# Fused bucketed attention and expert layer: block fills, routing operations, first weight buffer and last-pair order changed

## The chip, the cores and the metric

The kernel runs on one core of a Trainium2 chip. The metric is device microseconds (us) of one execution. The kernel before takes 723.25 us, the median of three runs (722.49 to 725.14).

## The reference

Two layers follow each other. The first is attention over 4 batches, 8 heads, 768 tokens and a head width of 64, in which a query sees a key only if both fall into the same of 64 buckets (six signs of random projections). The second sends each of the 3072 tokens (width 512) to one of 8 experts.

```python
q_bits = (np.einsum('bhsd,dk->bhsk', q, proj) > 0)
k_bits = (np.einsum('bhsd,dk->bhsk', k, proj) > 0)
mask = q_bucket[:, :, :, None] == k_bucket[:, :, None, :]
scores = np.where(mask, scale * (q @ k.T), -1e9)
attn = exp(scores - max) / (sum + 1e-9);  x = attn @ v      # then heads side by side: (3072, 512)

logits = x @ w_gate;  expert_idx = argmax(logits)            # first of equal ones
gate_w = softmax(logits)[expert_idx]
y = relu(x @ w1[expert_idx]) @ w2[expert_idx]
out = gate_w[:, None] * y
```

## The kernel before

**Pairs.** Attention goes over 16 pairs of heads, g = 0 to 15, four to a batch. A pair has 12 units of 128 queries (six score tiles to a head). A unit is a score on TensorE (`S`, lines 297 and 299), a minimum with eviction on VectorE (`R`, line 307) and an exponential on ScalarE (`X`, line 313). The probabilities of half of the units are transposed on TensorE (`T`, line 327) and evicted by ScalarE or VectorE (`E`, lines 377 and 375). Those of the other half are transposed in 32x32 blocks on VectorE (`D`, `blocks`, line 349). When the sixth of these is done, 16 DMAs on SP's queue put the blocks into place (`pt`, line 355), which the text calls the pair's **exchange**. `V` multiplies with the values (line 387), `O` evicts that, `K` is the product with the gate columns and an identity (line 407), `L` its eviction into the token rows `xr` (line 417). A minus behind a step means the pair before. So `V0-` of the next pair is what reads an exchange.

**The order of the work** is written out by hand. `HEAD` is pair 0, `PLAN` pairs 1 to 14 and `LAST` pair 15 with the first part of the expert layer. Each word issues its instructions on all engines and queues in program order, and every engine takes its own in that order.

**Empty blocks.** The sorted token rows lie in `sorted_rows`, one stretch for each expert. `fill(e)` (line 147) writes 512 empty rows (1156 KB) for expert e on SP's queue: for e up to 5 from the tile `C["empty"]`, for 6 and 7 by copying rows of expert 0. Blocks 0, 1 and 2 are issued in pair 0, and blocks 3 to 7 in step `I` of pairs 1 to 5, ahead of that pair's exchange.

**Routing.** `route` (line 427) finds each token's expert and slot, batch by batch, in pieces that the `R` steps of later pairs issue behind their own eviction. Batches 0 to 2 are routed whole (six tiles, in pairs 5 and 6, 9 and 10, 13 and 14). Batch 3 is routed in two halves, `r0` and `r1`, in `LAST`. Each has a matmul with a triangle of ones (line 458) that needs the one-hot experts (line 453). `scatter` (line 487) then writes the token rows by indirect DMA from GpSimd's (POOL's) queue.

**Weights.** The first expert's weights are split in two parts of lower precision in 16 pieces on POOL (`weights` and `weight_half`; lines 662 and 663, 906 and 912), four to a chunk. The chunks' buffers are the attention's own (`HOME`): w0 is also where the blocks of pair 14 wait for their exchange, w3 that of pair 13, w2 and w1 hold the last pair's queries and keys. `x`, `g`, `h` transpose the first expert's first 256 rows and split them (lines 749 to 753), `m` is the first product (`mm1`, line 770).

Of the kernel before, what the change touches and what calls it, by code (L numbers as in the profile page):

```python
# [12 lines left out]
OP = mybir.AluOpType  # L13
AX = mybir.AxisListType

B, H, S, D = 4, 8, 768, 64
# [3 lines left out]
NG = B * NP  # L20
# [11 lines left out]
M0 = float(2 ** 34)  # L32
# [22 lines left out]
def lsh_attention_moe(ctx, tc, qk, qk2, v, proj, wg, w1, w1p, w2, out):  # L55
    nc = tc.nc
# [88 lines left out]
    def fill(e):  # L145

        nc.sync.dma_start(xs[e * ROW:e * ROW + FILL].rearrange("(p j) w -> p j w", p=128),
                          C["empty"][:, 0:1].to_broadcast([128, FILL // 128, RW]) if e < 6 else
                          xs[:FILL].rearrange("(p j) w -> p j w", p=128))
# [190 lines left out]
    def blocks(i):  # L340

        g, r = divmod(i, 12)
        c, w = divmod(r, 2)
        if g not in ZT:
            ZT[g] = moe.tile([128, 4, 3, 2, NT * 32], F32, name="w0" if g == NG - 2 else "w3" if g % 2 else "w2"), []
        z, turned = ZT[g]
        turned.append(r)
        e = PP.pop(i).rearrange("p h c -> p (h c)").rearrange("p (k g j) -> p g k j", g=4, j=32)
        nc.vector.transpose(z[:, :, c, w].rearrange("p g (k i) -> p g k i", i=32), e)  # L349
        if len(turned) == 6:  # L350
            pt = pt_tile(2 * g)
            for r in range(4):
                for a in range(4):
                    q = (a + r) % 4
                    nc.sync.dma_start(pt[32 * q:32 * q + 32, a].rearrange("p t s k i -> p (t s k i)"),  # L355
                                      z[32 * a:32 * a + 32, q].rearrange("p c w x -> p (c w x)"))
            del ZT[g]

    def trans_ev(c, k, vec):

# [63 lines left out]
    def bc(ap):  # L424
        return ap[:, :, None].to_broadcast([128, ap.shape[1], E])

    def route(b, hfs):

        nt = 3 * len(hfs)
        l = wk.tile([128, 2, 2 * 3, E], F32, name="rl")  # L430
        lg, eq = l[:, 0, :nt], l[:, 1, :nt]
        f = wk.tile([128, 3, 2 * 3], F32, name="rf")
        mx, fi, sm = f[:, 0, :nt], f[:, 1, :nt], f[:, 2, :nt]
        oh = C["oh"] if nt > 3 else C["ohs"][:, hfs[0]]
        ex = C["ex"][:, 3 * hfs[0]:3 * hfs[0] + nt]
        dsc = C["desc"][:, None, :].to_broadcast([128, nt, E])
        many = nt > 3
        for i, hf in enumerate(hfs):
            nc.vector.tensor_reduce(lg[:, 3 * i:3 * i + 3], XR[b, hf][:, :, :GC].rearrange("p t (a x e) -> p t e a x", a=NP, e=E)[:, :, :, :, 0:PW // E:PW // E - 1], axis=AX.XY, op=OP.add)
            if many:  # L440
                yield
        nc.vector.tensor_reduce(mx, lg, axis=AX.X, op=OP.max)
        nc.vector.tensor_tensor(lg, lg, bc(mx), op=OP.subtract)
        if many:
            yield
        nc.vector.tensor_scalar(eq, lg, 0.0, None, op0=OP.is_equal)
        nc.vector.tensor_tensor(eq, eq, dsc, op=OP.mult)
        yield
        nc.vector.tensor_reduce(fi, eq, axis=AX.X, op=OP.max)
        nc.vector.tensor_tensor(eq, dsc, bc(fi), op=OP.subtract)  # L450
        if many:
            yield
        nc.vector.tensor_scalar(oh[:, :nt], eq, 0.0, None, op0=OP.is_equal)
        yield
        nc.scalar.activation(ex[:, :, 0:E], lg, AF.Exp)
        yield
        p = ps.tile([128, 512], F32, name="t", bufs=2)
        nc.tensor.matmul(p[:, :(nt + 1) * E], C["tri"], oh, start=True, stop=False)

        for t in range(nt):  # L460
            nc.tensor.matmul(p[:, (t + 1) * E:(nt + 1) * E], C["ones"], oh[:, t:t + 1, :].to_broadcast([128, nt - t, E]),
                             start=False, stop=(t == nt - 1))
        yield
        pb = wk.tile([128, 2 * 3 + 1, E], F32, name="pb")
        nc.vector.tensor_tensor(pb[:, :nt + 1], p[:, :(nt + 1) * E].rearrange("p (t e) -> p t e", e=E),
                                C["base"][:, None, :].to_broadcast([128, nt + 1, E]), op=OP.add)
        C["base"] = pb[:, nt]
        pb = pb[:, :nt]
        yield
        nc.vector.tensor_tensor(pb, pb, oh[:, :nt], op=OP.mult)  # L470
        slot = wk.tile([128, 2 * 3], I32, name="slot")
        with nc.allow_low_precision("whole numbers below 2**24"):
            nc.vector.tensor_reduce(slot[:, :nt], pb, axis=AX.X, op=OP.add)
        yield
        nc.vector.tensor_reduce(sm, ex, axis=AX.X, op=OP.add)
        for i, hf in enumerate(hfs):
            nc.vector.reciprocal(XR[b, hf][:, :, GC], sm[:, 3 * i:3 * i + 3])
            SL[b, hf] = slot[:, 3 * i:3 * i + 3]
        yield
# [15 lines left out]
    def go(r, n):  # L495
        for _ in range(n):
            next(r, None)
# [134 lines left out]


    CH, RAW = {}, {}
    HOME = "w0", "w3", "w2", "w1", "w4", "w5"
    P2 = {}

    def raw_load(c, a):
# [16 lines left out]
    def chunk_part(c, a):  # L655

        if a == 0:
            s = c % 6
            CH[c] = (moe if s < 4 else P2["p"]).tile([128, 2, 4, 512], F32R, name=HOME[s])
        w, r = CH[c], RAW[c, a // 2][:, a % 2]  # L660
# [118 lines left out]
    M1 = {}  # L779
# [115 lines left out]
    def weight_half(op, x):  # L895
# [35 lines left out]
    """.split()  # L931

    LAST = """
        S5 R5 S10 T31- R10 T30- S1 E31a- T32- nP tP nP tP E30a- E32a- X5 S0 S4 R4 X4 nP tP M1- R1 X1 V1- O1- T20 E20a
        R0 S2 nP T21 E21v T22 E22v R2 S3 X0 T00 E00a T01 E01a tP R3 S9 X2 T02 E02v R9 X9 S6 R6 X6 K1- L1- V0- O0- K0--
        L0-- S11 M0- S7 X3 T10 E10a M0 T11 E11v X10 S8 nP tP nP tP K0- L0- T12 E12a R8 R7 X8 X7 V0 O0 T31 E31a T30
        E30a T32 E32a R11 T40 E40a T41 E41v T42 E42v X11 T51 E51a M1 T50 T52 E50a K0 E52a V1 O1 L0 r0 r0 r0 r0 r0 r0
        K1 L1 r1 r1 r1 r1 r1 r1 r0 c0 r1 c1 x0 g0 h0 nP tP nP tP x2 g2 h2 m5 m3 u3 d3 u5 d5 m1 u1 d1 m0 u0 d0 m2 u2 d2
        m7 u7 d7 m4 u4 m6 u6 d6 d4
    """.split()  # L940

    SCAT = {}
# [1 line left out]
    steps = dict.fromkeys(range(B - 1), 0)  # L944

    def on(b, n):
        for _ in range(n):
            next(routes[b], None)
            steps[b] += 1

    def route_step(g, w, k):

        b, q = divmod(g - NP, NP)
        if 0 <= b < B - 1 and w[0] == "R" and q == 1 and {(g - 2, "L0"), (g - 2, "L1")} <= DONE and steps[b] < 7:
            if b not in routes:
                routes[b] = route(b, (0, 1))
            on(b, 1)
        if 0 <= b < B - 1 and q == 2:
            if w == "G":
                on(b, 9 - steps[b])  # L960
            elif w[0] == "R" and 9 <= steps[b] < 11:
                on(b, 1)
        s = {7: (0, 0), 8: (0, 1), 11: (1, 0), 12: (1, 1), 14: (2, 0)}.get(g)
        if w == "P7" and s:
            go(scatter(*s), 4)
        if g == NG - 1 and w[0] == "R" and k < 3:
            if k == 0:
                SCAT[0] = scatter(2, 1)
            go(SCAT[0], 1)
            if k == 2:  # L970
                rows(0)
# [27 lines left out]
    DONE = set()  # L999

    def step(g, w):

        n = g - w.count("-")
        w = w.rstrip("-")
# [5 lines left out]
        op, x = w[0], w[1:]  # L1010
# [12 lines left out]
            trans(6 * n + int(x[0]), int(x[1]))  # L1023
        elif op == "I":
            loads(n)
            if 0 < n < 6:
                fill(n + 2)
        elif op == "D" and n:
            blocks(12 * n + int(x))
        elif op == "E":  # L1030
# [63 lines left out]
    for g in range(NG):  # L1094
        peaks, since = 0, 0
        for w in HEAD if g == 0 else LAST if g == NG - 1 else PLAN:
            if w == "G":
                route_step(g, w, 0)
                since = 1
            step(g, w)  # L1100
            if g == 0 and w in ("z0", "z1"):
                fill(int(w[1]))
            if g == 0 and w == "w":
                fill(2)
            if w == "P7":
                route_step(g, w, 0)
            if w[0] == "R":
                route_step(g, w, peaks)
                if g == NG - 2 and 0 < since < 7 and steps[2] >= 9:
                    next(pick, None)  # L1110
                    since += 1
                    if since == 5:
                        raw_load(0, 0)
                        raw_load(0, 1)
                peaks += 1
            if g == NG - 1 and w == "c1":
                GT[0] = moe.tile([128, 4], F32, name="gate", bufs=3)
                nc.vector.tensor_copy(GT[0][:, :2], XG[0][:, :, GC])
                tokens(0)
# [30 lines left out]
    for n in range(1, len(PH)):  # L1150
        c0 = 4 * (PH[n][0] + 1)
# [91 lines left out]
```

## Time and profile before

| | |
|---|---|
| median of three runs | 723.25 us |
| the profiled execution | 723.71 us, span 721.9 us, mean granted TensorE clock 0.991 |
| TensorE (PE) busy | 97% of the span |
| VectorE (DVE), ScalarE (ACT), GpSimd (POOL) busy | 63%, 60%, 65% |
| chain that ended last, by engine | PE 82%, issue 5%, DVE 4%, DMA 3%, POOL 2%, ACT 2% |
| idle TensorE, by what ended it, in all | routing's one-hot (line 453) 5.3 us; row eviction (line 417) 3.6 us; line 387 after the eviction of line 377 3.0 us; masks 1.3 us |

With one engine busy nearly all the time, what remains is in the gaps of that engine. They are looked for in the list of waits and then, one by one, in order of time. A granted clock of 1.00 is 2.4 GHz and one of 0.50 is 1.2 GHz.

### The profile page before, as it was taken

Reading aid. Unit: us, or ns where it says so; the run is one execution under the profiler, and the core shown is the slowest. Engines: PE = TensorE matmul, PEld = TensorE weight load, DVE = VectorE, ACT = ScalarE, POOL = GpSimd, SP = SyncE. Lnnn points to the kernel's source line nnn. Section 1 sums busy time; section 2 is a strip of 40 time slices with the busy share of each in tenths; the row PEclk is TensorE's granted clock in tenths of the full one; section 3 lists DMA queues with packets and bytes.
Section 4 is the critical chain, followed back from the end, with each engine's and each line's share of the span. In section 5 each row is a group of like instructions: output and inputs, shape, how many; then the busy total and the mean of one; then the engine's idle time right before and its main releaser. Section 6 shows DMA issues by size and latency. Waiting matters only on the chain.

```text
span 721.9 us, 12253 instructions
## 1 busy us (share of the span) xinstructions
PE 697.0 (97%) x4219; PEld 570.3 (79%) x4219; DVE 456.6 (63%) x931; ACT 434.6 (60%) x864; POOL 468.0 (65%) x505
## 2 busy tenths in 40 slices
PE   8899999899999999999999699999999999999997
PEld 5777767767786768676876498899999999989896
DVE  8878777977878887788864723631757634262521
ACT  7988778677888788886865213544444444443320
POOL 7957745655887458874907854675666676768532
PEclk9999999999999999999999899999999999999999
DMA  7719878966787457864864236583637395747201
GB/s 287 209 33 263 204 219 203 230 186 161 207 218 218 132 140 221 226 204 115 242 187 164 94 132 172 196 231 126 166 123 189 132 124 188 193 148 201 88 11 40
DMA packets 64528, 123.09 MB, mean 171 GB/s; under 512 B 15331, under 2 KB 29027, under 8 KB 64400
## 3 DMA queue, kind: packets, MB, share of 16 engines
q1 hardware_dynamic: 56736, 103.17, 51.7%
q0 software_dynamic: 7584, 19.10, 8.9%
q8 instruction: 34, 0.56, 0.3%
q14 instruction: 30, 0.25, 0.1%
q10 hardware_dynamic: 144, 0.02, 0.0%
HBM read 65.75 MB, written 26.33 MB: 128 GB/s over the span
## 4 chain that ended last, share of the span: by engine, by line
PE 82%; issue 5%; DVE 4%; DMA 3%; POOL 2%; ACT 2%; SPq 2%; POOLq 0%; ACTq 0%
PE s L770 18%; PE t L387 17%; PE s L807 10%; PE s L297 8%; PE s L299 8%; PE t L327 8%; PE s L827 8%; PE t L407 3%; SPq L355 2%; DMA w<-masks 1%; PE t L254 1%; PE s L836 1%; ACT e L313 1%; DVE e L307 1%; DMA pt<-w 1%
## 5 line engine op out<-in xcount | busy, mean ns | idle before, releaser
L307 DVE TENSOR_SCALAR_CACHE_REDUCE e<-s 128x768 f32<-128x768 f32 x192 | 178.6, 953 | 65.6 <-PE s L299 56.6
L313 ACT ACTIVATE e<-e,m 128x768 f32<-128x768 f32 x192 | 177.9, 930 | 18.8 <-DVE e L307 16.6
L666 POOL TENSOR_TENSOR w<-raw,w 128x512 fp32r<-128x512 f32 x112 | 144.5, 1316 | 38.6 <-ACT w L665 38.1
L387 PE MATMUL t<-pt,vt 128*64 128x384 f32 x768 | 130.9, 490 | 4.0 <-ACT pt L377 3.0
L770 PE MATMUL s<-xh,w 128*128 128x456 f32 (+6 forms) x672 | 126.8, 346 | 0.0
L770 PEld LDWEIGHTS s<-xh,w 128*128 128x128 f32 x672 | 119.2, 188 | 3.1
L387 PEld LDWEIGHTS t<-pt,vt 128*64 128x64 f32 x768 | 53.6, 137 | 66.9 <-issue 55.2
L786 DVE SCALAR_TENSOR_TENSOR hh<-s,hh 128x256 fp32r<-128x256 f32 (+7 forms) x64 | 35.5, 555 | 109.3 <-ACT hh L784 103.9
L327 PE MATMUL t<-ident,e 128*128 128x128 f32 x648 | 92.7, 275 | 4.8 <-DVE xr L417 3.6
L377 ACT ACTIVATE pt<-t 128x512 f32<-128x512 f32 (+1 forms) x150 | 84.2, 582 | 17.9 <-PE t L327 16.4
L327 PEld LDWEIGHTS t<-ident,e 128*128 128x128 f32 x648 | 76.8, 141 | 13.1 <-ACT pt L377 4.0
L784 ACT ACTIVATE hh<-s 128x256 fp32r<-128x256 f32 (+7 forms) x64 | 31.4, 490 | 89.9 <-PE s L770 86.5
L349 DVE STREAM_TRANSPOSE w<-e 128x768 f32<-128x768 f32 x84 | 79.2, 966 | 0.2 <-ACT e L313 0.2
L807 PE MATMUL s<-hh,w 128*128 128x456 f32 (+3 forms) x384 | 74.9, 355 | 0.0
L807 PEld LDWEIGHTS s<-hh,w 128*128 128x128 f32 x384 | 71.1, 188 | 2.6
L665 ACT ACTIVATE w<-raw 128x512 fp32r<-128x512 f32 x112 | 66.3, 622 | 3.6 <-DMA raw<-in_w1p_dram 3.6
L843 POOL DMA_INDIRECT out_dram<-y,ix x26 | 25.9, 995 | 62.1 <-DVE y L841 30.9
L297 PE MATMUL s<-w 80*128 80x384 f32 x192 | 56.0, 373 | 2.2 <-DMA w<-masks 1.3
L827 PE MATMUL s<-w,hh 128*128 128x512 f32 (+1 forms) x240 | 56.4, 394 | 0.0
L297 PE MATMUL s<-qk 80*128 80x384 f32 x192 | 54.8, 367 | 0.0
L827 PEld LDWEIGHTS s<-w,hh 128*128 128x128 f32 (+1 forms) x240 | 44.6, 187 | 10.5
L299 PE MATMUL s<-w 128*128 128x384 f32 x192 | 50.0, 342 | 0.0
(205 smaller groups left out, 1000.1 us busy)
## 6 DMA issues: line engine op xcount, KB each, us to landing
pt<-w SPq DMA_DIRECT2D x224, 144.0 KB
raw<-in_w_dram SPq DMA_DIRECT2D x36, 512.0 KB
raw<-in_w1p_dram SPq DMA_DIRECT2D x28, 512.0 KB
xd<-in_qk_dram SPq DMA_DIRECT2D x14, 768.0 KB
sorted_rows<-xr SPq DMA_DIRECT2D x6, 1156.0 KB
vt<-in_v_dram SPq DMA_DIRECT2D x16, 384.0 KB
masks<-bits POOLq DMA_DIRECT2D x14, 192.0 KB, 3.8
sorted_rows<-sorted_rows SPq DMA_DIRECT2D x2, 1156.0 KB
```

The lines of the kernel that those rows point to most:

```text
L297: nc.tensor.matmul(p[:, a, :HALF], k[0:80, 2, c], k[0:80, 3, n], start=i >= 4, stop=i < 4)
L299: nc.tensor.matmul(p[:, a, :HALF], k[:, 0, c], k[:, 1, n], start=i < 4, stop=i >= 4)
L307: nc.vector.tensor_scalar(e, SC.pop(i)[:, :, :HALF], CEIL, None, op0=OP.min, op1=OP.min, accum_out=m)
L313: nc.scalar.activation(e, e, AF.Exp, bias=m, scale=-1.0, accum_out=SM[g, hf][:, t, s:s + 1])
L327: nc.tensor.transpose(o[:, j, w], e[w][:, kt // 3, (kt % 3) * 128:(kt % 3) * 128 + 128], ident)
L349: nc.vector.transpose(z[:, :, c, w].rearrange("p g (k i) -> p g k i", i=32), e)
L377: nc.scalar.activation(o, x, AF.Copy)
L387: nc.tensor.matmul(p[s * 64:(s + 1) * 64, :HALF], VT[g][:, kt, s, :], PT[u][:, :, :, s, kt].rearrange("p a t i -> p t a i"), start=(kt == ...
L666: nc.gpsimd.tensor_tensor(w[:, 1, a], r, w[:, 0, a], op=OP.subtract)
L770: nc.tensor.matmul(p[:, :c], w[:, a, d, fs], x[:, b, d, :c], start=(k == 0), stop=(k == 11))
L807: nc.tensor.matmul(p[:, :c], w[:, a, f % 4, ms], h[b][:, f, :c], start=(k == 0), stop=(k == 23))
L827: nc.tensor.matmul(p[:pw], HH[n][b][:, f, i:i + pw], w[:, a, f % 4], start=(k == 0), stop=(k == 23))
```

## The change

Four things change.

1. `fill(2)` leaves pair 0 and `fill(3)` to `fill(7)` leave step `I`. Instead `fill(g + 1)` is issued behind the 16 exchange DMAs of pairs 1 to 6.
2. `route` compares the logits with their maximum directly, and the order number with the found one directly, instead of a subtraction and a comparison with zero each. The subtraction that the exponential needs comes later, on POOL for batches 0 to 2 and on VectorE for batch 3. The pieces are one fewer for batches 0 to 2, and the counts in `route_step` and in the loop follow.
3. `HOME` begins with w3 instead of w0: the first chunk of weights goes to w3 and the second to w0.
4. `LAST` has a new order.

```diff
@@ blocks
             del ZT[g]
+            if g < 7:
+                fill(g + 1)
@@ route
         nc.vector.tensor_reduce(mx, lg, axis=AX.X, op=OP.max)
-        nc.vector.tensor_tensor(lg, lg, bc(mx), op=OP.subtract)
+        nc.vector.tensor_tensor(eq, lg, bc(mx), op=OP.is_equal)
         if many:
             yield
-        nc.vector.tensor_scalar(eq, lg, 0.0, None, op0=OP.is_equal)
         nc.vector.tensor_tensor(eq, eq, dsc, op=OP.mult)
-        yield
+        if not many:
+            yield
         nc.vector.tensor_reduce(fi, eq, axis=AX.X, op=OP.max)
-        nc.vector.tensor_tensor(eq, dsc, bc(fi), op=OP.subtract)
         if many:
             yield
-        nc.vector.tensor_scalar(oh[:, :nt], eq, 0.0, None, op0=OP.is_equal)
+        nc.vector.tensor_tensor(oh[:, :nt], dsc, bc(fi), op=OP.is_equal)
+        (nc.gpsimd if many else nc.vector).tensor_tensor(lg, lg, bc(mx), op=OP.subtract)
         yield
@@
-    HOME = "w0", "w3", "w2", "w1", "w4", "w5"
+    HOME = "w3", "w0", "w2", "w1", "w4", "w5"
@@ LAST
-        S5 R5 S10 T31- R10 T30- S1 E31a- T32- nP tP nP tP E30a- E32a- X5 S0 S4 R4 X4 nP tP M1- R1 X1 V1- O1- T20 E20a
...
+        S0 S1 R0 R1 T31- E31a- T30- E30a- M0- S5 R5 S6 X0 T32- E32a- nP tP X5 S4 R4 X4 X1 R6 X6 K0-- L0-- M1- V1- O1-
...
@@ step
             loads(n)
-            if 0 < n < 6:
-                fill(n + 2)
@@ loop
-            if g == 0 and w == "w":
-                fill(2)
```

SP's queue from pair 1's exchange to the loads behind pair 2's, before and now (`pt` is the exchange, `xd` and `vt` are loads of queries, keys and values, `sorted_rows` a block):

```order
L355 DMA pt<-w_521 32x1152 x16
L80 DMA xd<-in_qk_dram 128x1536
L84 DMA vt<-in_v_dram 128x768
L147 DMA sorted_rows<-xr 512x1x578
L355 DMA pt<-w_786 32x1152 x16
L80 DMA xd<-in_qk_dram 128x1536
```

```order
L355 DMA pt<-w_520 32x1152 x16
L147 DMA sorted_rows<-xr 512x1x578
L80 DMA xd<-in_qk_dram 128x1536
L84 DMA vt<-in_v_dram 128x768
L355 DMA pt<-w_785 32x1152 x16
L147 DMA sorted_rows<-xr 512x1x578
L80 DMA xd<-in_qk_dram 128x1536
```

The block stands behind the exchange instead of ahead of it, and the load of the next queries and keys stands behind both, as it did.

POOL's queue in pair 5, before and now (`qk`, `xd` are the next pair's operands, `masks` their mask rows, `rl` the logits):

```order
L198 TENSOR_TENSOR qk<-xd,qk 64x768
L194 CAST qk<-xd 64x768
L196 COPY qk<-qk 64x768
L270 DMA qk<-masks 16x4x384 x2
L200 TENSOR_TENSOR qk<-xd,qk 64x768
L198 TENSOR_TENSOR qk<-xd,qk 64x768
L200 TENSOR_TENSOR qk<-xd,qk 64x768
```

```order
L198 TENSOR_TENSOR qk<-xd,qk 64x768
L194 CAST qk<-xd 64x768
L196 COPY qk<-qk 64x768
L455 TENSOR_TENSOR rl<-rl,rf 128x48
L270 DMA qk<-masks 16x4x384 x2
L200 TENSOR_TENSOR qk<-xd,qk 64x768
L198 TENSOR_TENSOR qk<-xd,qk 64x768
L200 TENSOR_TENSOR qk<-xd,qk 64x768
```

The subtraction stands ahead of the mask DMAs and of three long operations.

TensorE's queue at the end of attention, before and now (line 407 and now 409 is `K`, 387 and now 389 `V`, 458 to 461 and now 460 to 463 the routing matmuls, 751 the transposes of the first expert's rows):

```order
L407 MATMUL t<-wgt,ot 128x144 x3
L387 MATMUL t<-pt,vt 64x384 x12
L458 LDWEIGHTS tri
L458 MATMUL t<-ohs,tri 128x32
L461 LDWEIGHTS ones
L461 MATMUL t<-ohs,ones 128x24
L461 LDWEIGHTS ones
L461 MATMUL t<-ohs,ones 128x16
L461 LDWEIGHTS ones
L461 MATMUL t<-ohs,ones 128x8
L407 MATMUL t<-wgt,ot 128x144 x3
```

```order
L409 MATMUL t<-wgt,ot 128x144 x3
L389 MATMUL t<-pt,vt 64x384 x12
L460 LDWEIGHTS tri
L460 MATMUL t<-ohs,tri 128x32
L463 LDWEIGHTS ones
L463 MATMUL t<-ohs,ones 128x24
L463 LDWEIGHTS ones
L463 MATMUL t<-ohs,ones 128x16
L463 LDWEIGHTS ones
L463 MATMUL t<-ohs,ones 128x8
L751 MATMUL s<-ident,xd 128x128 x4
L409 MATMUL t<-wgt,ot 128x144 x3
```

Half of the row transposes now stand between the first routing matmuls and the last `K`; the other half stands earlier, ahead of the last three groups of `T`. Before, all eight stood behind the second routing matmuls.

## Rows read from the trace of the kernel before

**Rows 1.** The page, busy time: engine, busy us, share, instructions.
```profile
PE 697.0 (97%) x4219; PEld 570.3 (79%) x4219; DVE 456.6 (63%) x931; ACT 434.6 (60%) x864; POOL 468.0 (65%) x505
```

**Rows 2.** Waits, 30 to 360 us: us in total, times, longest us.
```profile
PE t L327 <- DVE xr L417: 3.6, 3, 2.1
PE t L387 <- ACT pt L377: 3.0, 2, 1.6
PE s L297 <- DVE e L307: 0.9, 2, 0.6
PE t L387 <- ACT e L313: 0.4, 1, 0.4
...
POOL xd L1055 <- PE t L254: 48.8, 13, 8.0
```

**Rows 3.** Timeline of pair 0 and the first score of pair 1: start, us, what.
```profile
14.13 2.74 SPq L147 DMA_DIRECT2D sorted_rows<-xr  x3
...
29.92 0.58 PE L297 MATMUL s<-w 80*128 80x384 f32 x2 [1.31 <-DMA w<-masks]
```

**Rows 4.** Timeline, `V0-` in pairs 3 and 5, and ACT beside the latter.
```profile
95.71 4.09 PE L387 MATMUL t<-pt,vt 128*64 128x384 f32 x24 [1.57 <-ACT pt L377]
...
146.02 4.09 PE L387 MATMUL t<-pt,vt 128*64 128x384 f32 x24
...
146.28 0.58 ACT L377 ACTIVATE pt<-t 128x512 f32<-128x512 f32 x1
```

**Rows 5.** Timeline of SP's queue: an exchange with a block ahead, one without.
```profile
76.33 13.07 SPq L355 DMA_DIRECT2D pt<-w  x16
...
175.99 11.12 SPq L355 DMA_DIRECT2D pt<-w  x16
```

**Rows 6.** Timeline of pair 5: routing on DVE, POOL beside it, and PE.
```profile
135.83 1.42 DVE L443 TENSOR_TENSOR rl<-rl,rf 128x48 f32<-128x48 f32 x1
...
139.06 1.81 POOL L200 TENSOR_TENSOR qk<-xd,qk 64x768 fp32r<-64x768 f32 x1
...
139.07 1.87 DVE L447 TENSOR_TENSOR rl<-rl,desc 128x48 f32<-128x48 f32 x1
...
141.60 1.57 PE L327 MATMUL t<-ident,e 128*128 128x128 f32 x8 [2.06 <-DVE xr L417]
...
142.48 0.21 DVE L450 TENSOR_TENSOR rl<-desc,rf 128x48 f32<-128x48 f32 x1
```

**Rows 7.** Windows: stretch, PE, PEld, DVE, ACT, POOL busy (instructions), PEclk, DMA share, GB/s.
```profile
143.00:144.00 1.00, 1.00 (x5) 1.00 (x5) 1.00 (x4) 1.00 (x5) 0.00 (x0) 0.50 0.25 98
```

**Rows 8.** Timeline of pair 9: POOL's mask DMAs, routing on DVE, and PE.
```profile
230.95 1.09 POOL L270 DMA_DIRECT2D qk<-masks  x2
...
234.18 1.63 DVE L443 TENSOR_TENSOR rl<-rl,rf 128x48 f32<-128x48 f32 x1
...
238.69 1.06 PE L327 MATMUL t<-ident,e 128*128 128x128 f32 x8 [0.80 <-DVE xr L417]
```

**Rows 9.** Timeline of pair 15: POOL's first piece of weights.
```profile
378.38 0.61 POOL L662 CAST w<-raw 128x512 fp32r<-128x512 f32 x1 [16.20 <-DMA pt<-w]
```

**Rows 10.** Timeline of PE, from the last transposes to the first product.
```profile
393.48 6.16 PE L327 MATMUL t<-ident,e 128*128 128x128 f32 x36
...
405.79 0.19 PE L458 MATMUL t<-ohs,tri 128*128 128x32 bf16 x1 [1.15 <-DVE ohs L453]
...
411.50 0.18 PE L458 MATMUL t<-ohs,tri 128*128 128x32 bf16 x1 [4.11 <-DVE ohs L453]
...
411.61 1.95 PE L749 MATMUL s<-ident,xd 128*128 128x128 f32 x8
```

**Rows 11.** Groups on DVE, 396 to 430 us: busy us, mean ns, idle us before.
```profile
L450 DVE TENSOR_TENSOR rl<-desc,rf 128x24 f32<-128x24 f32 x2 | 1.8, 917 | 0.1
...
L753 DVE TENSOR_TENSOR xhe<-s,xhe 128x512 fp32r<-128x512 f32 x2 | 1.3, 682 | 0.0
...
L453 DVE TENSOR_SCALAR ohs<-rl 128x24 bf16<-128x24 f32 x2 | 1.0, 511 | 0.1
L446 DVE TENSOR_SCALAR rl<-rl 128x24 f32<-128x24 f32 x2 | 1.0, 502 | 0.1
```

More of the change, by code (lines that the diff above doesn't have):

```diff
@@ L933, in lsh_attention_moe @@
     LAST = """
-        S5 R5 S10 T31- R10 T30- S1 E31a- T32- nP tP nP tP E30a- E32a- X5 S0 S4 R4 X4 nP tP M1- R1 X1 V1- O1- T20 E20a
[L935 to L939, printed above, removed]
+        S0 S1 R0 R1 T31- E31a- T30- E30a- M0- S5 R5 S6 X0 T32- E32a- nP tP X5 S4 R4 X4 X1 R6 X6 K0-- L0-- M1- V1- O1-
+        T20 E20v S2 nA tP T21 E21v nP tP S10 T22 R2 E22a S8 nP tP R10 T01 E01a T00 E00a X10 S3 X2 T02 R3 E02v R8 X8 nP
+        tP S7 V0- O0- nP tP K1- L1- K0- L0- nP S9 X3 T10 E10a T11 E11v M0 S11 tP nP tP T12 E12a V0 R7 X7 R11 X11 O0
+        T50 E50a T51 E51a T52 E52a R9 T31 E31a T30 T32 E30v E32v x0 X9 M1 T40 E40a T41 E41v T42 K0 g0 h0 E42a V1 L0 r0
+        r0 r0 r0 r0 r0 r0 c0 x2 O1 K1 L1 r1 r1 r1 r1 r1 r1 r1 c1 g2 h2 m6 m3 u3 d3 m2 u2 d2 m7 u6 d6 u7 d7 m1 u1 d1 m4
+        u4 d4 m0 u0 d0 m5 u5 d5
     """.split()
@@ L953, in route_step @@
         b, q = divmod(g - NP, NP)
-        if 0 <= b < B - 1 and w[0] == "R" and q == 1 and {(g - 2, "L0"), (g - 2, "L1")} <= DONE and steps[b] < 7:
+        if 0 <= b < B - 1 and w[0] == "R" and q == 1 and {(g - 2, "L0"), (g - 2, "L1")} <= DONE and steps[b] < 6:
             if b not in routes:
@@ L959, in route_step @@
             if w == "G":
-                on(b, 9 - steps[b])
-            elif w[0] == "R" and 9 <= steps[b] < 11:
+                on(b, 8 - steps[b])
+            elif w[0] == "R" and 8 <= steps[b] < 10:
                 on(b, 1)
@@ L1108, in lsh_attention_moe @@
                 route_step(g, w, peaks)
-                if g == NG - 2 and 0 < since < 7 and steps[2] >= 9:
+                if g == NG - 2 and 0 < since < 7 and steps[2] >= 8:
                     next(pick, None)
```

## The prediction

> **What bounds the kernel now.** The busy times come first [rows 1]. TensorE works 697.0 of 721.9 us and no other engine more than two thirds, so work on the others costs nothing unless TensorE waits for it. What can be won is TensorE's idle time, about 25 us, and what its clock loses around it. So I read TensorE's waits next, and then each long one in order of time. They sit in four places.
>
> *Pair 1's first score* waits 1.31 us for its mask rows [rows 3]. The three blocks of empty rows were issued at 14.13 us, ahead of the masks.
>
> *`V0-`* waits in several early pairs. The list names an eviction by ACT twice, for 3.0 us, and an exponential once, for 0.4 us [rows 2]. The eviction only looks guilty. In pair 5 `V0-` begins at 146.02 us and that same eviction at 146.28 us [rows 4], so `V0-` does not need it. What it does need is the exchange, and in these pairs the exchange stands behind a block of empty rows.
>
> *Routing of batches 0 to 2* holds up a row eviction (line 417) three times, 3.6 us in all [rows 2]. In pair 5 the subtraction takes 1.42 us and the multiplication 1.87 us, while the second subtraction, of the same shape, takes 0.21 us [rows 6]. The multiplication starts 0.01 us behind a POOL operation of 1.81 us and ends with it. So a small VectorE operation waits until POOL's current one is over. In pair 5 TensorE then idles 2.06 us and its clock falls to 0.50 [rows 7], which is 1.2 GHz: eight transposes take 1.57 us there [rows 6] and 1.06 us at full clock [rows 8].
>
> *The end of attention* waits 1.15 us and 4.11 us for the one-hot matrices of `r0` and `r1` [rows 10]. The clock falls again: eight row transposes take 1.95 us [rows 10].
>
> The Trainium skill (SBUF — State Buffer, Who interferes with whom) says that VectorE and GpSimd share a pair of ports as an exclusive lock, that whoever starts first blocks the other, and that reductions never take part. By that rule a subtraction on POOL is one more holder of the lock, which speaks against the second part of this change. It would not alter the sum below, which takes new waits from the lengths of POOL's old operations.
>
> **The change, part by part.**
>
> *Blocks of empty rows.* Nothing is added in number; they are moved on SP's queue. One leaves pair 0, so a third of the transfers queued before the masks goes, and I take the 1.31 us as gone, with 0 as the other end in case the masks themselves are slow. In pairs 1 to 5 the exchange no longer has a block ahead. With a block its 16 DMAs take 13.07 us to issue and without 11.12 us [rows 5], 1.95 us less, which covers the longest wait, 1.57 us [rows 4]. I take 3.0 + 0.4 = 3.4 us [rows 2] as gone, with 0.4 us as the lower end if ACT is the true cause. The next load of queries and keys now follows exchange and block instead of block and exchange, the same bytes, except in pairs 1 and 6, where a block is new. That makes it later by some 2 us there. POOL reads it, and POOL waits for TensorE 13 times for 48.8 us [rows 2], 3.8 us in the mean, so this is hidden; without that cover it would cost at most those 2 us twice. Later scatters find all blocks written about a pair earlier. **Blocks: 4.7 us (0.4 to 4.7).**
>
> *Routing, batches 0 to 2.* In pair 5 the comparison with zero goes, and the multiplication runs directly behind its `R`, so the row eviction is no longer behind a blocked pair of operations. I take the 2.06 us as gone. From the transposes at 141.60 us to `V0-` at 146.02 us [rows 6, 4] 4.4 us pass, the larger part at half clock; without the idle time the clock should hold, worth an estimated 1.5 us (2.2 us if all of it was at half). What is late next is the last comparison (one-hot). POOL's subtraction waits for the first comparison, and the mask DMAs and three long operations behind it slide by as much, so a 1.81 us operation [rows 6] now lies where the last comparison runs. `R` of the next unit follows later, and I charge TensorE 1.0 us for its score buffer. Pair 5: 2.06 + 1.5 - 1.0 = 2.6 us. In pairs 9 and 13 the other two waits go, 3.6 - 2.06 = 1.5 us, and the 0.9 us of waits for `R` [rows 2] become two of 1.0 us: 1.5 + 0.9 - 2.0 = 0.4 us. **Routing: 3.0 us (0 to 6.0; the upper end has no new wait, 2.06 + 1.5 + 1.5 + 0.9).** The exponential waits for POOL's subtraction, which is over an `R` step earlier; costed at nothing, and covered by ACT's 40% of idle time.
>
> *First chunk to w3.* POOL idles 16.20 us, to 378.38 us, until pair 14's exchange has left w0 [rows 9]. w3 was left a pair earlier, so four pieces can be done before. TensorE waits for none of this, so by itself it is worth 0. It matters only through the lock: POOL ends its 16 pieces earlier, perhaps before `r1`.
>
> *New order of the last pair.* TensorE's work is the same. The nine last groups of transposes take 6.16 us for 36 [rows 10], 0.17 us each against 1.06 / 8 = 0.13 us in a run without a full buffer [rows 8], so 1.4 us are lost to evictions. The new order has four matmuls of another buffer among them and shares their evictions out otherwise; I take 0.5 us (-1.0 to 1.4; a worse order can lose about as much as this one does).
>
> At the end three things change. Each chain to a one-hot loses the comparison with zero, 0.50 us, and merges subtraction and comparison, another 0.51 us [rows 11]: 1.0 us. If POOL is already done, the operation of line 450 also falls from 0.92 us [rows 11] to about 0.21 us [rows 6], another 0.7 us. `r0`'s wait falls by 1.0 of its 1.15 us. `r1`'s falls by 1.0 to 1.7 us; I take 1.35, in the middle, because POOL's finish falls between the two chains. The eight row transposes no longer run at half clock behind `r1`: 1.95 - 1.06 = 0.9 us. The first product still finds the clock low, and its second half of rows is split only behind the rest of `r1`: `h2` takes 0.68 us [rows 11] after some small operations. The 0.3 us wait it replaces and the matmuls that can already run pay for that: 0. **Last pair: 0.5 + 1.0 + 1.35 + 0.9 = 3.7 us (1.0 to 6.0; the lower end has neither the order's nor `r0`'s part and half the rest, the upper end keeps the clock up as well).**
>
> **Sum.** 4.7 + 3.0 + 0 + 3.7 = 11.4 us less than the profiled execution's 723.71 us (span 721.9 us, 1.8 us around it): 712.3 us. The profiled execution lies 0.46 us above the median of the runs, so I forecast **711.9 us** against 723.25 us. Behind the first product nothing waits on the old times, so what is won stays won.
>
> **The rivals.**
>
> *The end does not move.* POOL's pieces still lie over `r1`, each operation that vanishes leaves the next one blocked, and the new order loses elsewhere what it gains. For it: the operations of line 450 take 0.92 us under POOL's pieces [rows 11], and shortening a chain between locks only moves the wait. Against it: two operations fewer cannot be made up wholly by one. The last pair then gives 0, and the time is 711.9 + 3.7 = 715.6 us. Chance 0.18.
>
> *The routes do not move.* The last comparison's new wait in pair 5 is as long as the old one and drops the clock too. Then routing gives 0: 711.9 + 3.0 = 714.9 us. For it: POOL's three long operations slide just there. Against it: `R` stands between them and the score buffers are three. Chance 0.12. The Trainium skill (Perfetto Trace Analysis, Optimizing Scalar/DVE Operations) says that work handed from VectorE to GpSimd may not help, since they share a port; by that rule this is the likelier case.
>
> *`V0-` waits for ACT after all*, as the list says. Then 3.0 of the 3.4 us stay: 714.9 us. Chance 0.05; pair 5 speaks against it [rows 4].
>
> *More comes than forecast.* The clock holds through the end of attention and the last comparison meets no lock: 2.3 us at the end and 3.0 us in the routes more: 706.6 us. Chance 0.08.
>
> *Slower.* The subtraction on POOL holds the mask DMAs behind it until the first comparison is done. In pair 9 the masks were issued at 230.95 us and the comparison's predecessor ran at 234.18 us [rows 8], so 3.2 us at least. If the next pair's first score waited for that and the clock fell, each of three pairs would lose 3.2 + 2.2 = 5.4 us, 16.2 us in all: 711.9 + 16.2 = 728.1 us. It decides only if the masks have less slack than 3.2 us and their landing; they were issued 7.7 us ahead of the transposes at 238.69 us [rows 8] and are read in the next pair. Chance 0.03.
>
> **How the numbers follow.** The forecast keeps the remaining 0.54. Its own bounds and the first three rivals reach from about 707 to 717 us; two of the rivals together would give 718.6 us and lie outside, as do the last two. A measurement of this kernel tells 0.5% from no change, 3.6 us, so faster means below 719.6 us. The forecast and four rivals end there; I leave 0.07 for the first two rivals together with a loss that I don't see, and 0.03 for slower.
>
> **What would show it.** Right, if in the changed profile pair 1's wait for masks and the waits of `V0-` are gone, line 417 holds TensorE in none of pairs 5, 9 and 13, the granted clock stays at 1.00 in pair 5, and the wait before the second routing matmuls is between 2.3 and 3.2 us. Wrong, if `V0-` still waits in pairs 2, 3 and 6, if the waits for `R` in pairs 5, 9 and 13 grow beyond 1.0 us each, or if a wait of over 1 us stands anywhere in the new last pair before `V1`.

## The result, and the profile after

The changed kernel takes **715.41 us** in the median (715.13 to 716.06), against 723.25 us before: a ratio of 0.9894 with an interval of 0.9866 to 0.9921. The forecast was 711.9 us, with a range of 707 to 717 us. The profiled execution takes 715.56 us, of which the span is 713.7 us, 8.2 us less than before. The page's busy times and TensorE's waits between 30 and 360 us answer to [rows 1, 2]:

```profile
PE 695.7 (97%) x4219; PEld 568.3 (80%) x4219; DVE 454.3 (64%) x924; ACT 434.9 (61%) x864; POOL 469.0 (66%) x507
...
PE s L297 <- DVE e L307: 2.9, 2, 1.6
PE t L327 <- DVE xr L419: 2.7, 1, 2.7
```

Line 417 is now line 419, line 387 is line 389. The waits of `V0-` for ACT and for the exponential, 3.4 us before, are no longer in the list. The row eviction (line 419) still is: once instead of three times, but for longer. And the waits for `R` (line 307) grew from 0.9 to 2.9 us. So the waits that the blocks were to end are gone, and the routing still holds TensorE up.

A table of pair lengths says it in full. A pair is counted from the start of its projection matmuls (line 254) on PE's timeline to that of the next, and "end" from pair 14's to the last instruction. A pair without routing takes 23.08 us when TensorE waits for nothing. The kernels below the line are the experiments. Beside the groups of experiments the kernel before took 722.15 to 723.82 us, and each ratio is to the runs of its group.

| us | pairs 1 to 4 and 6, sum | pair 5 | pair 9 | pair 13 | end | median of the runs |
|---|---|---|---|---|---|---|
| before | 120.03 | 27.54 | 25.21 | 25.60 | 380.35 | 723.25 |
| changed | 115.05 | 29.42 | 25.27 | 25.59 | 376.14 | 715.41 |
| | | | | | | |
| blocks alone | 115.35 | 25.08 | 25.22 | 25.36 | 380.23 | 715.64 |
| routing alone | 118.98 | 28.22 | 25.27 | 25.60 | 380.11 | 725.69 |
| last pair and w3 alone | 122.07 | 25.29 | 25.22 | 25.19 | 376.46 | 719.78 |
| subtraction on VectorE | 115.09 | 25.05 | 25.16 | 25.72 | 375.39 | 712.02 |
| subtraction in the next pair | 115.08 | 24.89 | 25.01 | 24.96 | 375.86 | 712.19 |
| w0 back | 115.04 | 28.22 | 25.29 | 25.60 | 380.11 | 720.17 |
| old order back | 115.04 | 29.39 | 25.25 | 25.61 | 378.70 | 718.33 |
| POOL's operations exchanged | 115.07 | 28.08 | 25.25 | 25.59 | 376.60 | 716.20 |
| routing behind POOL | 115.07 | 23.73 | 23.73 | 23.74 | 377.49 | 708.02 |
| the same, subtraction on VectorE | 115.07 | 23.74 | 23.73 | 23.74 | 375.38 | 707.67 |
| the same on POOL, product before `r1` | 115.07 | 23.73 | 23.74 | 23.74 | 372.04 | 703.56 |

Of the 8.2 us of span, pairs 1 to 4 and 6 give 4.98, the end 4.21 and the start 0.91 (the first projection starts at 10.52 instead of 11.43 us, ahead of all that was changed; in the thirteen traces this start lies between 10.52 and 12.37 us). Pair 5 takes back 1.88 us. The blocks alone take 715.64 us, within 0.3 us of the four parts together.

**Pair 5.** Its timeline, VectorE's and POOL's rows first and then PE's, answers to [rows 6, 7]:

```profile
131.55 0.21 DVE L445 TENSOR_TENSOR rl<-rl,rf 128x48 f32<-128x48 f32 x1
...
131.91 0.27 POOL L455 TENSOR_TENSOR rl<-rl,rf 128x48 f32<-128x48 f32 x1 [3.50 <-DVE rl L445]
132.34 1.02 POOL L270 DMA_DIRECT2D qk<-masks  x2 [0.17 <-issue]
...
132.90 4.17 DVE L448 TENSOR_TENSOR rl<-rl,desc 128x48 f32<-128x48 f32 x1
...
133.38 1.86 POOL L200 TENSOR_TENSOR qk<-xd,qk 64x768 fp32r<-64x768 f32 x1
135.17 1.81 POOL L198 TENSOR_TENSOR qk<-xd,qk 64x768 fp32r<-64x768 f32 x1
...
137.96 1.94 PE L327 MATMUL t<-ident,e 128*128 128x128 f32 x8 [2.70 <-DVE xr L419]
```

POOL reached its new subtraction (line 455) early and waited 3.50 us for the first comparison. That comparison is free now, 0.21 us. But the mask DMAs and the long operations, which stand behind the subtraction, start only then, right where the multiplication (line 448) runs. It takes 4.17 us, through the rest of a mask DMA issue and two long operations, where before it took 1.87 us behind one [rows 6]. The row eviction stands behind it, TensorE idles 2.70 us, and the granted clock is 0.50 from 138 to 144 us. A window of each stretch at the lower clock, this one and the end of attention (columns as in [rows 7]; 0.50 is the clock):

```profile
141.00:142.00 1.00, 1.00 (x5) 1.00 (x4) 0.58 (x1) 1.00 (x3) 0.00 (x0) 0.50 0.03 9
408.00:409.00 1.00, 1.00 (x6) 1.00 (x6) 0.00 (x0) 0.00 (x0) 0.79 (x3) 0.50 0.18 53
```

**Pairs 9 and 13.** The multiplication is free, and the last comparison is caught instead. POOL, VectorE and TensorE in pair 9, to set beside [rows 8]:

```profile
230.54 0.27 POOL L455 TENSOR_TENSOR rl<-rl,rf 128x48 f32<-128x48 f32 x1 [3.53 <-DVE rl L445]
...
232.08 1.88 POOL L200 TENSOR_TENSOR qk<-xd,qk 64x768 fp32r<-64x768 f32 x1
...
233.54 2.27 DVE L454 TENSOR_TENSOR oh<-desc,rf 128x48 bf16<-128x48 f32 x1
...
233.88 1.85 POOL L198 TENSOR_TENSOR qk<-xd,qk 64x768 fp32r<-64x768 f32 x1
...
236.74 0.62 PE L297 MATMUL s<-w 80*128 80x384 f32 x2 [1.27 <-DVE e L307]
```

In pair 13 it takes 2.60 us. `R` stands behind it, and TensorE waits 1.27 and 1.59 us for that (the 2.9 us in the list). Both pairs are as long as before.

**The end of attention**, PE's timeline, to set beside [rows 10]:

```profile
400.85 0.19 PE L460 MATMUL t<-ohs,tri 128*128 128x32 bf16 x1 [0.42 <-DVE ohs L454]
...
404.98 0.18 PE L460 MATMUL t<-ohs,tri 128*128 128x32 bf16 x1 [2.37 <-DVE ohs L454]
...
405.08 1.18 PE L772 MATMUL s<-xhe,w 128*128 128x256 f32 x7
407.40 4.87 PE L772 MATMUL s<-xhe,w 128*128 128x256 f32 x28 [1.14 <-DVE xhe L755]
```

The waits for `r0` and `r1` fell from 1.15 and 4.11 us to 0.42 and 2.37 us. A new one of 1.14 us, for `h2`, stands behind the first seven matmuls. The clock is at 0.50 for some 3.5 us instead of 10.

### The profile page after: what moved, and what is told of

It is laid out like the page before. It is cut to its first block, busy times and chain, and to the rows that moved or that the text cites. A ratio compares the mean times of both kernels' runs of the same rounds, so it can differ in the third digit from the quotient of the medians.

```text
span 713.7 us, 12263 instructions
## 1 busy us (share of the span) xinstructions
PE 695.7 (97%) x4219; PEld 568.3 (80%) x4219; DVE 454.3 (64%) x924; ACT 434.9 (61%) x864; POOL 469.0 (66%) x507
## 4 chain that ended last, share of the span: by engine, by line
PE 89%; issue 4%; DVE 3%; ACT 1%; POOL 1%; DMA 0%; POOLq 0%; ACTq 0%; DVEq 0%
PE s L772 18%; PE t L389 18%; PE s L809 10%; PE s L297 10%; PE t L327 10%; PE s L299 9%; PE s L829 8%; PE t L409 3%; PE t L254 2%; PE s L838 1%; DVE e L307 1%; POOL w L668 1%; DVE rl L448 1%; PE t L103 1%; ACT e L313 0%
```

## The experiments

**Where the subtraction stands.** Two versions of the changed kernel; the first takes POOL out, the second moves POOL's subtraction behind the pair's long operations.

```diff
-        (nc.gpsimd if many else nc.vector).tensor_tensor(lg, lg, bc(mx), op=OP.subtract)
+        nc.vector.tensor_tensor(lg, lg, bc(mx), op=OP.subtract)
```

> The changed kernel with the subtraction of batches 0 to 2 back on VectorE, all else as changed. Theory (the subtraction on POOL waits 3.5 us for the first comparison and so slides the mask DMAs and three long POOL operations onto the multiplication and the last comparison): POOL's operations return to where they lay before, 2.4 us earlier in pair 5. There the first comparison is blocked for some 1.3 us again, the multiplication for 1 us at most instead of 4.17 us, line 419 holds TensorE for under 1 us instead of 2.70 us, and the pair falls from 29.42 us to about 25 us. Pairs 9 and 13 gain nothing (25.2 to 25.6 us), since the first comparison is blocked there as in the kernel before. Total 711 us. Rival (the shorter routing itself, its multiplication directly behind an R, meets POOL wherever the subtraction is): pair 5 stays at 29 us and the total at 715 us. Second rival (the pair's earlier exchange is to blame): the same, 715 us.

```diff
-        (nc.gpsimd if many else nc.vector).tensor_tensor(lg, lg, bc(mx), op=OP.subtract)
+        if not many:
+            nc.vector.tensor_tensor(lg, lg, bc(mx), op=OP.subtract)
         yield
+        if many:
+            nc.gpsimd.tensor_tensor(lg, lg, bc(mx), op=OP.subtract)
         nc.scalar.activation(ex[:, :, 0:E], lg, AF.Exp)
@@ route_step: the rest runs at the next pair's G
-        ... and steps[b] < 6:
+        ... and steps[b] < 5:
```

> The changed kernel with the subtraction still on POOL, but issued with the exponential at the start of the next pair, behind the pair's long POOL operations. Theory (its place in POOL's queue costs, not the engine): the pairs are as in the version with the subtraction on VectorE, pair 5 at about 25 us, pairs 9 and 13 at 25.2 to 25.6 us; total 711 us. Rival (any subtraction on POOL blocks VectorE's routing through the shared lock): pair 5 at 29 us, total 715 us.

Measured: 712.02 us (ratio to before 0.9851, 0.9802 to 0.9901) and 712.19 us (0.9850, 0.9802 to 0.9899), pair 5 at 25.05 and 24.89 us. The rivals of both expectations fall. It is the place in POOL's queue that costs: the same operation on the same engine, one pair later, costs nothing. VectorE and POOL in pair 5 of the version with the subtraction on VectorE:

```profile
132.13 1.84 POOL L198 TENSOR_TENSOR qk<-xd,qk 64x768 fp32r<-64x768 f32 x1
...
132.45 1.60 DVE L445 TENSOR_TENSOR rl<-rl,rf 128x48 f32<-128x48 f32 x1
...
134.05 1.83 POOL L200 TENSOR_TENSOR qk<-xd,qk 64x768 fp32r<-64x768 f32 x1
...
134.85 1.10 DVE L448 TENSOR_TENSOR rl<-rl,desc 128x48 f32<-128x48 f32 x1
```

Each is caught by one long operation and let go at its end. TensorE's three waits for line 419 are 2.3 us in sum, none above 0.8 us.

**The routing where POOL is idle.** If VectorE is late because it is held up behind POOL's operations, the three steps should be free once those are over. This edit is made to the second version.

```diff
-        ... and steps[b] < 5:
+        ... and steps[b] < 5 and (
+                steps[b] < 2 or w in ("R1", "R6", "R7")):
```

> As the version with the subtraction at the start of the next pair, but the three steps with small VectorE operations wait for the R units R1, R6 and R7, behind POOL's three long operations, which end 16 us into pairs 9 and 13 and 18 us into pair 5. Theory: none of the three operations is blocked (0.2 to 0.35 us each), line 419 and R hold TensorE nowhere in these pairs, the clock stays at 1.00, and pairs 5, 9 and 13 take about 24 us each, the 23.1 us of a plain pair and 0.9 us for the routing matmuls and their wait. Total about 707 us. Rival (the waits in pairs 9 and 13 come from the order of the pair and not from the lock): pairs 9 and 13 stay at 25.3 us and the total at 710 us or above. Second rival (the one-hot now comes too late): a wait of over 1 us before the routing matmuls, and the total at 713 us.

Measured: 708.02 us (0.9786, 0.9737 to 0.9836), all three pairs at 23.73 or 23.74 us. VectorE's rows of pair 5:

```profile
138.38 0.21 DVE L445 TENSOR_TENSOR rl<-rl,rf 128x48 f32<-128x48 f32 x1
...
140.34 0.20 DVE L448 TENSOR_TENSOR rl<-rl,desc 128x48 f32<-128x48 f32 x1
...
141.57 0.20 DVE L454 TENSOR_TENSOR oh<-desc,rf 128x48 bf16<-128x48 f32 x1
```

None is held up, and the routing matmuls start without a wait. The theory holds for all three pairs; both rivals fall. So 1.5 and 1.9 us of pairs 9 and 13 had come from POOL's operations too. (The end is 2 us longer in this run than in the next version's: the clock is at 0.50 for longer behind `r1`'s wait.)

> The version with the routing behind POOL's long operations, with the subtraction on VectorE. Theory (the engine of the subtraction is worth nothing once no lock is in the way): pairs 5, 9 and 13 at 23.7 us each as with POOL, total 707 to 708 us. Rival (0.2 us of VectorE at the start of a pair are on the path to the routing matmuls, so POOL does save something): some 0.2 us more in each of the three pairs, 708.5 us.

That version, with `nc.vector` in place of the second version's `nc.gpsimd`, takes 707.67 us (0.9809, 0.9784 to 0.9833) with the same pairs. Once nothing is held up, the engine of the subtraction is worth nothing that can be measured. POOL's help was not needed.

**Each part alone**, on the kernel before. First the blocks:

```diff
             del ZT[g]
+            if g < 7:
+                fill(g + 1)
...
-            if 0 < n < 6:
-                fill(n + 2)
...
-            if g == 0 and w == "w":
-                fill(2)
```

> The kernel before with the blocks of empty rows alone moved behind each pair's exchange. Theory (V0- waited for the exchange behind a block, pair 1's score for masks behind three): pair 1's 1.31 us and 3.4 us of waits of V0- go, pairs 1 to 4 and 6 take 0.94, 0.50, 1.62, 0.34 and 1.58 us less as in the changed kernel, pairs 5, 9 and 13 stay as before; 4.7 us off, 718.5 us. Rival (part of these waits went with the start or with the rest of the change): less than 3 us off, over 720 us.

Measured: 715.64 us (0.9906, 0.9877 to 0.9935). Pairs 1 to 4 and 6 give 4.68 us, as the theory says (pair 1 gives 0.86 us of it, and 0.43 us of its wait for masks are left here). But pair 5 gives 2.46 us more, with the old routing. POOL's first mask DMAs of pair 5, in the kernel before and with the blocks alone:

```profile
134.27 1.02 POOL L270 DMA_DIRECT2D qk<-masks  x2 [1.56 <-DMA masks<-bits]
```

```profile
128.67 1.02 POOL L270 DMA_DIRECT2D qk<-masks  x2
```

Before, POOL waited there until the sign bits had been written to memory, so its long operations slid onto the multiplication. Without blocks in the way it waits for nothing, and the pair is as pair 9. The 2.06 us of [rows 6] were the blocks' doing. This stood in the trace of before and was read as the routing's.

Then the routing (the edits of `route` and `route_step`, and the count in the loop):

> The kernel before with the shorter routing alone (subtraction on POOL as in the changed kernel), blocks, buffers and the order of the last pair as before. Theory (the blocks alone shorten pair 5, since their transfers no longer delay the masks that POOL waits for there; the routing's slide makes the same pair longer): the waits of V0- stay, pair 5 goes from 27.54 us to about 29.4 us as in the changed kernel, since the subtraction and not the masks sets POOL's place there, and the end loses 2 to 3 us through the shorter chains to the one-hots. Total 722 us. Rival (the routing gains its 2.06 us wait as forecast and something else in the changed kernel takes it back): pair 5 at 25 us, total 718 us.

Measured: 725.69 us, 0.3% slower than before (1.0029, 1.0004 to 1.0053), 3.7 us above the expectation. The profiled execution is at the fast end (724.07 us, of 723.51 to 729.29), so its pairs do not show what the longer ones lose. Pair 5 went up, though by 0.7 us and not 1.9; the rival falls. The multiplication takes 4.18 us and TensorE waits 2.72 us there, as in the changed kernel; behind that the clock is at 0.50 for some 3.5 us, and in the changed kernel for some 7 us, which is the missing 1.2 us. The end, however, gained 0.24 us instead of 2 to 3: VectorE reaches the one-hots of `r0` and `r1` sooner (waits of 0.24 and 2.81 us), but the clock is at 0.50 afterwards all the same, and the first product then waits 1.37 us for `h2`, where the wait before was 0.34 us.

Then the last pair's order and w3, with the old routing:

> The kernel before with the new order of the last pair and the first chunk in w3, nothing else. Theory (as forecast, order and lock are worth little without the shorter chains): 0.5 us for the order, up to 0.7 us because POOL is done earlier, 722 us; the waits for r0 and r1 stay above 4 us in sum. Rival (the order brings most of the 4.2 us that the end gained): 719 us, and the span behind pair 14's first projection falls from 380.35 us to about 376 us.

Measured: 719.78 us (0.9937, 0.9905 to 0.9969); the end takes 376.46 us. The rival was right: 3.9 of the 4.2 us come without the shorter chains. Undoing one of the two in the changed kernel tells which:

```diff
-    HOME = "w3", "w0", "w2", "w1", "w4", "w5"
+    HOME = "w0", "w3", "w2", "w1", "w4", "w5"
```

> The changed kernel with the first chunk's buffer back in w0, the rest as changed. Theory (w3 acts only through the lock, in that POOL's pieces end before the last routing): POOL idles for w0 again and its pieces lie over r1's small operations, which are blocked for some 0.7 to 2 us; 716.5 us. Rival (w3 is worth nothing, POOL catches up): 715.4 us. Second rival (the early nP tP of the new order then stand in front of POOL's other work until w0 is free): a new wait of TensorE in the last pair and over 718 us.

> The changed kernel with the old order of the last pair, the rest as changed. Theory (0.5 us for the evictions of the last transposes, 0.9 us for the eight row transposes that stand at half clock behind r1 again, and POOL's last four pieces come behind r1 instead of ahead): 717 us. Rival (the order alone carries the end's gain): 719 us, the end as long as before. Pair 5 stays at 29 us in any case.

With w0 back: 720.17 us (0.9934, 0.9908 to 0.9960), the end at 380.11 us, the whole gain gone. With the old order (the old `LAST` in place of the new): 718.33 us (0.9902, 0.9872 to 0.9933), the end at 378.70 us, 2.6 us of the gain gone, between theory and rival. So the order is worth nothing while the first chunk is in w0 (380.11 us with either order), w3 is worth 1.4 us with the old order (380.11 to 378.70 us), and the two together 4.0 us. One trace stands behind each figure, and the same last pair took from 375.38 to 377.49 us in the traces of six kernels, so the 1.4 us is not sure. The new order also gives the rounding of one of the sixteen pieces to ScalarE (`nA` in place of one `nP`), which the list of changes does not name and no run takes apart. POOL's last piece of weights, the one-hot of `r1` and PE's wait for it with w0 back:

```profile
406.70 0.92 DVE L454 TENSOR_TENSOR ohs<-desc,rf 128x24 bf16<-128x24 f32 x1
...
407.67 0.18 PE L460 MATMUL t<-ohs,tri 128*128 128x32 bf16 x1 [3.56 <-DVE ohs L454]
...
410.13 1.27 POOL L665 TENSOR_TENSOR w<-raw,w 128x512 fp32r<-128x512 f32 x1
```

POOL's pieces run until 411.40 us there, over both chains; in the changed kernel the last one ends at 400.75 us, 0.1 us ahead of `r0`'s matmuls, and `r1`'s comparisons and its product take 0.18 us each. The first expectation had the mechanism and too small a size. A wait of 1.06 us for an eviction in the transposes comes too, so the second rival, a new wait in the last pair and over 718 us, has a part in it.

**Two POOL operations in a row.** In the changed kernel a caught operation waited for two in pairs 5, 9 and 13; in the kernels whose subtraction does not stand ahead of POOL's long operations it waited for one. The expectation puts that down to a gap between POOL's operations.

```diff
-        T51 E50a R1 N E51a S7 X4 S6 T52 D5 R6 X1 E52a V0- P3 R7 P2 I D4 M0- P7 X6 X7 O0- D1
+        T51 E50a R1 N E51a S7 X4 S6 T52 D5 R6 X1 E52a V0- P2 R7 P3 I D4 M0- P7 X6 X7 O0- D1
```

> The changed kernel with POOL's first two long operations of each pair exchanged (line 198 ahead of line 200); the subtraction stays where the change put it. In the trace of the changed kernel line 198 starts 0.07 us before line 200 ends, while the next line 200 starts 0.1 us behind line 198. Theory (the small VectorE operation that was caught lost the lock to two POOL operations in a row because no gap lies between them): with line 198 first there is a gap, so the multiplication in pair 5 is blocked for 2.4 us at most instead of 4.17 us and the last comparisons in pairs 9 and 13 for 0.3 to 0.8 us instead of 2.27 and 2.60 us; pair 5 at 26.5 to 27.5 us, pairs 9 and 13 at 23.7 to 24.5 us, total 711 us. Rival (the caught operation waits for two operations whatever lies between them): the pairs as in the changed kernel, total 715.4 us.

Measured: 716.20 us (0.9922, 0.9898 to 0.9946), pairs 9 and 13 as in the changed kernel, pair 5 at 28.08 us. POOL and VectorE in pair 5, and a window behind it:

```profile
134.50 4.18 DVE L448 TENSOR_TENSOR rl<-rl,desc 128x48 f32<-128x48 f32 x1
...
135.00 1.86 POOL L198 TENSOR_TENSOR qk<-xd,qk 64x768 fp32r<-64x768 f32 x1
136.80 3.69 POOL L200 TENSOR_TENSOR qk<-xd,qk 64x768 fp32r<-64x768 f32 x2
```

```profile
143.00:144.00 1.00, 1.00 (x9) 0.80 (x10) 0.66 (x2) 1.00 (x3) 0.25 (x1) 1.00 0.03 8
```

The multiplication is held as long as in the changed kernel and TensorE waits as long (2.71 us); pair 5 is 1.3 us shorter because the clock is back at 1.00 sooner. The time is near what the rival said, but the experiment does not decide. The exchanged second operation again starts 0.06 us before the first ends, so the gap that was to be made is not there. The kernel before says that a missing gap is not enough. There the subtraction of pair 5 [rows 6] was caught by the first of these two and was over at 137.25 us, 0.06 us behind that one's end, though the second had started 0.03 us ahead of it:

```profile
135.35 1.84 POOL L200 TENSOR_TENSOR qk<-xd,qk 64x768 fp32r<-64x768 f32 x1
137.16 1.83 POOL L198 TENSOR_TENSOR qk<-xd,qk 64x768 fp32r<-64x768 f32 x1
```

What makes the caught operation wait for a second one stays open.

**A version that beats both.** On the version with the routing behind POOL, the idle time at `r1` is filled with the first product.

```diff
-        r0 r0 r0 r0 r0 r0 c0 x2 O1 K1 L1 r1 r1 r1 r1 r1 r1 r1 c1 g2 h2 m6 m3 u3 d3 m2 u2 d2 m7 u6 d6 u7 d7 m1 u1 d1 m4
+        r0 r0 r0 r0 r0 r0 c0 x2 O1 g2 K1 h2 L1 r1 r1 r1 m6 r1 r1 r1 r1 c1 m3 u3 d3 m2 u2 d2 m7 u6 d6 u7 d7 m1 u1 d1 m4
```

> The version with the routing behind POOL's long operations, and at the end of attention the second half of rows is split (g2, h2) and the first product's matmuls for m6 are issued ahead of the routing matmuls of r1. Theory (the wait of 2.37 us for r1's one-hot and of 1.14 us for h2 are idle time that these twelve matmuls can fill): the first wait falls below 1 us, the second goes, and the clock at 0.50 behind them gets shorter or goes; 2.6 to 4.3 us less, 704 to 705.5 us. Rival (h2 of 0.68 us delays r1's chain on VectorE by as much, and the clock falls all the same): under 1 us less, 707.5 us.

Measured: **703.56 us** (703.17 to 703.80), a ratio to before of 0.9747 (0.9724 to 0.9769). PE's timeline:

```profile
393.95 1.68 PE L775 MATMUL s<-xhe,w 128*128 128x256 f32 x12
396.83 0.18 PE L463 MATMUL t<-ohs,tri 128*128 128x32 bf16 x1 [1.19 <-DVE ohs L454]
...
396.93 5.27 PE L775 MATMUL s<-xhe,w 128*128 128x256 f32 x42
```

The time is a little below the expected range. The wait for `r1` falls to 1.19 us, a little above the expectation; the one for `h2` is gone, and the clock stays at 1.00 through the end of attention, as in this window:

```profile
397.00:398.00 1.00, 1.00 (x13) 1.00 (x10) 0.78 (x5) 0.13 (x1) 0.97 (x1) 1.00 0.76 290
```

The end takes 372.04 us, 5.4 us less than in the trace without the edit; the medians differ by 4.5 us. That is more than the 2.3 us by which the two waits shrink. The rest is put down to the clock, which was at 0.50 for some 7 us in the trace without the edit.

## Why the prediction was right in its sum, and not in its terms

The forecast was 3.5 us too low, inside its range. Of its own signs, three came true: pair 1's wait for masks and the waits of `V0-` are gone, and the wait before the second routing matmuls is 2.37 us. The row eviction holding TensorE in no pair and the clock at 1.00 in pair 5 did not, and the waits for `R` grew past 1.0 us, which was to show it wrong. Against its terms:

- **Blocks, 4.7 us forecast; 7.1 us.** The places it named gave what it said in sum, 4.68 us in pairs 1 to 4 and 6, though pair 1 gave 0.86 us instead of 1.31 and the pairs with `V0-` 3.82 us instead of 3.4. `V0-` needed the exchange and not ACT. What it left out is pair 5: another 2.46 us, since POOL's masks there came late behind the blocks too. The step "the 2.06 us as gone" was booked under routing; it belongs here.
- **Routing, 3.0 us gain forecast; a loss of 4.3 us in pair 5.** This is the step that failed: "In pair 5 the comparison with zero goes, and the multiplication runs directly behind its `R`, so the row eviction is no longer behind a blocked pair of operations." Against the blocks alone, pair 5 goes from 25.08 to 29.42 us, and pairs 9 and 13 stay within 0.25 us. Some 1.2 us of the 4.3 hang on how long the clock stayed down (28.1 to 28.2 us in three other kernels with the same wait), and with the old blocks the loss was 0.7 us. The prediction knew that POOL's operations would slide by as much as the subtraction waits, and put them where the last comparison runs. In pairs 9 and 13 that was so, at 1.27 and 1.59 us instead of 1.0 us each. In pair 5 they met the multiplication, with two operations' blocking instead of the 1.0 us charged. The rival "the routes do not move" was the nearest, and it too was on the hopeful side in pair 5. With the subtraction on VectorE the shorter routing is worth nothing either (25.05, 25.16 and 25.72 us against 25.08, 25.22 and 25.36 us).
- **Work handed to POOL.** The Trainium skill (Perfetto Trace Analysis, Optimizing Scalar/DVE Operations) says that such a move may not help because of the shared port, and the prediction gave that case 0.12. The result agrees with it. But the runs put the cause elsewhere: not the 0.27 us operation's share of the port, but its wait of 3.5 us at the head of POOL's queue.
- **First chunk to w3, 0 by itself; 4.0 us given the new order.** "Perhaps before `r1`" was the larger part. POOL ended at 400.75 us instead of 411.40 us. With the old order w3 gave perhaps 1.4 us.
- **Last pair, 3.7 us; 4.2 us.** The size was right and the make-up wrong. The shorter chains, priced at 2.35 us, gave 0.24 us alone: the two waits shrank by 2.2 us, but the first product then waited 1.0 us longer for `h2`, and the clock stayed down as long. Order and w3 gave 3.9 us without them. `h2`, set at zero, costs a wait of 1.14 us. No wait of over 1 us stands in the new last pair ahead of `V1`.
- **The clock.** The forecast of 1.00 in pair 5 failed with its wait. At the end it falls later and for some 3.5 us instead of 10. The forecast had the first product find it low; its first seven matmuls still ran at 1.00.

So it was luck that the sum came so near. Two errors of opposite sign met: routing 3.0 + 4.3 = 7.3 us too good, and blocks, end and start 2.4 + 0.5 + 0.9 = 3.8 us too poor; the difference is the 3.5 us of the forecast's miss, to a rounding, and the 0.9 us of the start are chance.

## What to carry to other kernels

Before an operation is put on a queue that has room, ask when its input is there and what stands behind it: its own time was 0.27 us, its wait slid 6.5 us of other work under the operations that TensorE waits for. Where one engine's long operations hold up another's small ones, moving the small ones to where the first is idle can be worth more than making them fewer: here it gave some 1.3 us in pair 5, where the smaller number gave nothing. And a wait should be followed back over all its engines: [rows 6] show what VectorE was held by, but why POOL was there at that time was one row further.

## What was not expected of the hardware

- A small VectorE operation that was held up by a POOL operation did not always get its turn when that one ended. In the changed kernel it waited through two in a row in each of pairs 5, 9 and 13 (4.17, 2.27 and 2.60 us), and with them exchanged again (4.18 us in pair 5). With the subtraction on VectorE it waited for one (1.60 and 1.10 us). The Trainium skill (SBUF — State Buffer, Who interferes with whom) says that whoever starts first blocks the other for the whole instruction. The traces agree for one operation; that the one held up can lose a second time, to an instruction that starts after it, is what these rows add.
- POOL's row for the mask DMAs is two issues of some 0.5 us. In pair 5 of the changed kernel the multiplication started 0.05 us into the second (at 132.85 us) and was held to its end and beyond. In pairs 9 and 13 it started in the first (231.00 to 231.56 and 325.82 to 326.38 us) and took 0.20 us, past the start of the second in pair 9. What decides between them was not tried.
- The same wait did not cost the same. Behind a wait of 2.70 to 2.72 us in pair 5 the clock was at 0.50 for some 7 us in two kernels (changed, old order back) and for some 3.5 us in three (routing alone, w0 back, POOL's operations exchanged), and the pair took 29.4 us in the first two and 28.1 to 28.2 us in the others. Why is open.
- In the three kernels with the old blocks, the first seven pairs take 163.9, 163.7 (last pair and w3 alone) and 163.5 us (routing alone) in sum, though pair 5 varies by 2.9 us and pair 6 by 4.4 us among them; with the blocks alone moved it is 156.4 us. So where a stall was taken in one pair, another was spared. That a queue of transfers sets the pace of this stretch is a reading of the sums, not shown by itself.
